# Attention gradients for one query: an eighth of the stores of V's gradient moved to GpSimd's DMA queue

## The chip, the cores and the metric

The kernel runs on one core of a Trainium2 chip. The metric is the device time of one execution in microseconds (us); the runs before the change have a median of 1301.13 us (three runs, 1300.45 to 1303.02). The core has five engines with their own instruction streams: TensorE (PE in the profile; its weight loads are PEld), VectorE (DVE), ScalarE (ACT), GpSimd (POOL) and SyncE (SP). Its 16 DMA engines move data between the device memory (HBM) and the on-chip memory (SBUF, 128 rows called partitions). A DMA is issued by SP, ACT or POOL and is split over the DMA engines; the profile names the queue by its issuer (SPq, ACTq).

## The reference: what is computed

For each of 2 x 32 heads there is one query q, and 8192 keys and values of 128 numbers, in bf16. The forward pass is

```
scores = q . k / sqrt(128);  p = softmax(scores);  out = sum of p * v
```

and the kernel returns `out` and the three gradients of it for a given `grad_out`: dq (as small as q), dk and dv (each as large as k and v, 134 MB). So 268 MB are read and 268 MB written, and there is little arithmetic for each byte. For one head, with dS = p * (grad_out . v - delta): dv is the outer product of p and grad_out, dk that of dS and q (scaled), and dq the sum of dS * k.

## The kernel before, in words

The 64 heads are handled as 32 pairs. K of a pair is one SBUF tile of 4 MB, [128 partitions, 128 positions, 128 numbers]; partitions 0 to 63 hold one head, 64 to 127 the other. V of the pair is another such tile. One partition is 32 KB of contiguous device memory.

There are six such buffers (`ring`, 24 MB), so three pairs are on the chip at a time. The gradients are written in place: once V of a pair is used up, dV (outer product of the row grad_out and the weights p) is written over V, and dK over K (`outer`, L275, on VectorE). Then the buffer is stored (`store`, L283, issued by ScalarE), and when the store has landed, SP loads K or V of the pair three later into it (`load`, L108). dV of pair g sits in the buffer that K of pair g+3 takes, and dK of g in the one that V of g+3 takes.

The order of all work is written out by hand. The outer loop runs over h, the pair that is being read in; the inner loop over 16 steps j, 8 chunks of K and then 8 of V. At each step TensorE transposes a chunk (L119), ScalarE or VectorE copies the result out (`ev`, L126 and L124), and TensorE multiplies it by the query or by grad_out (L136). Pair h-1 is finished in the same steps: its step number ("slot") is s = j + 16. In slots 12 to 17 dV is written, in slot 18 (j = 2 of the next pair) it is stored; in slots 19 to 23 dK is written and in slot 24 (j = 8) stored. Directly after each store's issue in program order stands the load of the pair three later, on SP's queue. SP works through its queue in order, and each load waits there for the store of its buffer to land. The last pair is stored in eight parts (1 MB each) as it is finished.

GpSimd does nothing in the loop: it prepares constants and clears two weight tiles (`wz`, L295) at the start. No DMA is issued by it.

Of the kernel before, what the change touches and what calls it, by code (L numbers as in the profile page):

```python
# [11 lines left out]
BF16 = mybir.dt.bfloat16  # L12
# [2 lines left out]
CH = 16  # L15
HC = CH // 2
RING = 6


@with_exitstack  # L20
def kernel(
# [11 lines left out]
    nc = tc.nc  # L33
    B, H, Sq, D = q.shape
    Sk = k.shape[2]
    P = nc.NUM_PARTITIONS
# [4 lines left out]
    NT = 2 * Sk // P  # L41
# [6 lines left out]
    const = ctx.enter_context(tc.tile_pool(name="const", bufs=1))  # L48
# [18 lines left out]
    q_rows = q.rearrange("b h s d -> (b h s) d")  # L67
# [4 lines left out]
    def by_pairs(x):  # L72
        rows = x.rearrange("b h s d -> (b h s) d")
        return rows.rearrange("(g p n) d -> g p n d", p=P, n=NT)

    k_v, v_v, dk_v, dv_v = (by_pairs(x) for x in (k, v, out_2, out_3))
# [8 lines left out]

    ring = [kvp.tile([P, NT, D], BF16, name=f"ring{i}") for i in range(RING)]
    acc = ps_one.tile([P, 4 * D], F32, name="acc", tag="acc")
# [12 lines left out]
    pairs = [Pair() for _ in range(NP)]  # L100
# [6 lines left out]
    def load(g, w):  # L107
        nc.sync.dma_start(out=pairs[g].kv[w][:], in_=(k_v, v_v)[w][g])  # L108
# [4 lines left out]
    def transposes(g, j, u):  # L113
        x = pairs[g]
        w, c = divmod(j, NCH)
        tp = ps_tp.tile([P, HC, P], F32, name="tp", tag="tp")
        for i in range(HC):
            n = c * CH + u * HC + i
            nc.tensor.matmul(  # L119
                tp[:, i, :], lhsT=x.kv[w][:, n, :], rhs=ident_bf[:], start=True, stop=True  # L120
            )
        ev = evp.tile([P, HC, P], BF16, name="ev", tag="ev")
        if (j, u) in ((8, 0), (9, 0), (10, 0), (11, 0)):
            nc.vector.tensor_copy(out=ev[:], in_=tp[:])  # L124
        else:
            nc.scalar.copy(out=ev[:], in_=tp[:])  # L126
        x.ev[j, u] = ev

    def products(g, j, u):
        x = pairs[g]  # L130
        w, c = divmod(j, NCH)
        ev = x.ev.pop((j, u))
        cols = (qT_all, doT_all)[w][:, 2 * g : 2 * g + 2]
        for i in range(HC):
            n = c * CH + u * HC + i
            nc.tensor.matmul(  # L136
                scores(w)[:, :, n], lhsT=ev[:, i, :], rhs=cols, start=True, stop=True
            )

    def spread_row(g, w):  # L140
        pb = misc[:, (2 + w) * D : (3 + w) * D]
        for s, hs in enumerate(halves):
            nc.tensor.matmul(  # L143
                pb[hs],
                lhsT=ident_bf[0:BH, 2 * g + s : 2 * g + s + 1].to_broadcast([BH, HP]),
                rhs=nat[:, 1 - w, :],
                start=True,
                stop=True,
            )
        x = pairs[g]  # L150
        x.row = rowp.tile([P, D], BF16, name="row", tag="row")
        nc.scalar.copy(out=x.row[:], in_=pb)  # L152

    def row_max(x):
        x.mp = work.tile([P, 1], F32, name="mp", tag="mp")
        for s, hs in enumerate(halves):
            nc.vector.reduce_max(out=x.mp[hs], in_=scores(0)[hs, s, :], axis=AX.X)  # L157

    def all_max(x):
        mT = sm[0:1, 2 * NT : 2 * NT + P]  # L160
        nc.tensor.transpose(mT, x.mp[:], ident_f[:])
        x.gm = work.tile([1, 2], F32, name="gm", tag="gm")
        nc.vector.reduce_max(out=x.gm[:], in_=mT.rearrange("o (s p) -> o s p", s=2), axis=AX.X)

    def exps(x):
        mb = sm[:, 2 * NT + P : 2 * NT + P + 2]
        nc.tensor.matmul(mb, lhsT=ones_row[:], rhs=x.gm[:], start=True, stop=True)  # L167
        negm = work.tile([P, 1], F32, name="negm", tag="negm")
        x.E = big.tile([P, NT], F32, name="E_f", tag="E_f")
        x.ld = work.tile([P, 2], F32, name="ld", tag="ld")  # L170
        for s, hs in enumerate(halves):
            nc.vector.tensor_scalar(
                out=negm[hs], in0=mb[hs, s : s + 1], scalar1=-scale, scalar2=None, op0=ALU.mult
            )
        for s, hs in enumerate(halves):
            nc.scalar.activation(  # L176
                out=x.E[hs],
                in_=scores(0)[hs, s, :],
                func=ACT.Exp,
                bias=negm[hs],  # L180
                scale=scale,
                accum_out=x.ld[hs, 0:1],
            )

    def sums(x, w):
        x.lsum = (dp if w else sm)[:, 2 * NT + P + 8 : 2 * NT + P + 9]
        nc.tensor.matmul(x.lsum, lhsT=block[:], rhs=x.ld[:, w : w + 1], start=True, stop=True)  # L187
# [72 lines left out]
    def combine(g):  # L260
        x = pairs[g]
        c = misc[:, 0:4]
        for j in range(4):
            nc.tensor.matmul(  # L264
                c, lhsT=x.accsb[:, j * D : (j + 1) * D], rhs=pick[:, j],
                start=(j == 0), stop=(j == 3),
            )
        nc.vector.tensor_copy(  # L268
            out=colsT[:, :, 2 * g : 2 * g + 2], in_=c.rearrange("p (w s) -> p w s", w=2)
        )  # L270

    def outer(x, w, c):
# [6 lines left out]
            op=ALU.mult,  # L279
        )  # L280

    def store(g, w, a=0, b=NT):
        nc.scalar.dma_start(  # L283
            out=(dv_v, dk_v)[w][g][:, a:b, :], in_=pairs[g].kv[1 - w][:, a:b, :]
        )

    def outer_and_store(g, w, c):
        outer(pairs[g], w, c)
        if g == NP - 1 and c % 2:
            store(g, w, (c - 1) * CH, (c + 1) * CH)  # L290

    for i, src in enumerate((q_rows, do_rows)):
        nc.scalar.dma_start(out=nat[:, i, :], in_=src)
    for t in wz:
# [12 lines left out]
    STORE = {18: 0, 24: 1}  # L307

    with tc.manual_schedule():
        for g in range(RING // 2):  # L310
            load(g, 0)
            load(g, 1)
        for h in range(NP + 1):
            y = pairs[h] if h < NP else None
            x = pairs[h - 1] if h else None
            for j in range(NS):
                at = [(z, zg, s) for z, zg, s in ((x, h - 1, j + NS), (y, h, j)) if z]
                for u in range(2):
                    if y:
                        transposes(h, j, u)  # L320
                    if y and j:
                        products(h, j - 1, u)
                    elif x and j == 0:
                        products(h - 1, NS - 1, u)
                    if u == 0:
                        if y and j == 8:
                            spread_row(h, 0)
                        if x and j == 2:
                            spread_row(h - 1, 1)
                        if x and j == 8:  # L330
                            combine(h - 1)
                    else:
                        if y and j == 9:
                            all_max(y)
                        if y and j == 10:
                            exps(y)
                        if y and j == 11:
                            sums(y, 0)
                        if x and j == 1:
                            sums(x, 1)  # L340
                    if u == 1:
                        for z, zg, s in at:
                            for w, when in ((0, ACC_V), (1, ACC_K)):
                                for c in when.get(s, ()):
                                    weighted_rows(z, w, c)
                if y and j == 8:
                    row_max(y)
                if y and j == 11:
                    weights_v(y)
                if x and j == 0:  # L350
                    deltas(x)
                if x and j == 1:
                    weights_k(x)
                for z, zg, s in at:
                    if s in STORE and zg < NP - 1:
                        store(zg, STORE[s])
                        if zg + 3 < NP:
                            load(zg + 3, STORE[s])
                    for w, when in ((0, OUT_V), (1, OUT_K)):
                        for c in when.get(s, ()):  # L360
                            outer_and_store(zg, w, c)
                if x and j == 6:
                    acc_to_sbuf(x)
        for w, dst in enumerate((o_rows, dq_rows)):
            tps = ps_tp.tile([BH, P], BF16, name="tps", tag="tp")
            nc.tensor.transpose(tps[:], colsT[:, w, :], ident_bf[:])
            rows = evp.tile([BH, D], BF16, name=f"rows{w}", tag="ev")
            nc.scalar.copy(out=rows[:], in_=tps[:])
            nc.scalar.dma_start(out=dst, in_=rows[:])


# [28 lines left out]
```

## Time and profile before

| what | before |
|---|---|
| runs, median (lowest to highest) | 1301.13 us (1300.45 to 1303.02) |
| the profiled execution's own time | 1301.66 us |
| its span (first to last instruction) | 1299.9 us |
| PE, DVE, ACT, POOL busy | 84%, 72%, 70%, 0% of the span |
| HBM read, written | 268.47 MB, 268.47 MB (413 GB/s over the span) |
| loads on SP's queue, stores on ACT's | 64 of 4 MB; 62 of 4 MB and 8 of 1 MB |

How to read it: the profile's page has a line for each engine with its busy share in 40 equal slices of the span, given as digits (9 is 90% or more); the line "DMA" is the mean busy share of the 16 DMA engines. The "chain that ended last" follows the last instruction back to whatever released it, step by step, and gives the shares of the span by engine and line. "SPq L108 <- DMA out_dram<-ring" means that SP's queue, at line 108, waited for a DMA that stores a ring buffer. For DMA issues the page gives the median time from issue to landing. The trace also holds, for each transfer, the times of the sixteen increments of its semaphore, and for each packet (a contiguous run that one DMA engine moves) its queue, start, duration and size, without the name of the DMA engine. A view by windows gives, for a stretch of time, the busy time of each engine, the granted TensorE clock, the DMA engines' share and the GB/s moved.

### The profile page before, as it was taken

What the parts mean: (1) busy time and instruction counts of PE and PEld (TensorE: products, weight loads), DVE (VectorE), ACT (ScalarE), POOL (GpSimd) and SP (SyncE); (2) the same over time, 40 slices, a digit from 0 to 9 for tenths busy, and PEclk for the clock granted to TensorE, in tenths of its full rate; (3) what the DMA queues carried; (4) which work ended last, traced back from release to release, by engine and by line L of the source; (5) the groups of instructions that cost most, each with busy time, mean ns of one, the idle gap of its engine ahead of it and who ended that gap; (6) DMA issues with size and microseconds to landing.
All of it is one profiled execution on the core that took longest, in us unless ns stands there. A gap on an engine that the chain in (4) does not pass through costs nothing.

```text
span 1299.9 us, 42160 instructions
## 1 busy us (share of the span) xinstructions
PE 1093.5 (84%) x19044; PEld 936.6 (72%) x19044; DVE 930.0 (72%) x1355; ACT 906.3 (70%) x1091; POOL 2.0 (0%) x10
## 2 busy tenths in 40 slices
PE   4999899988888889888888887898888988889883
PEld 3777787776777778777677776677677877778771
DVE  0888788767867677767786676776677666776775
ACT  4887778767866678757686576876578666786761
POOL 0000000000000000000000000000000000000000
PEclk9999989889988788868898688988788777887876
DMA  9999999999999999999999999999999999999986
GB/s 404 417 425 424 429 427 432 427 430 430 429 429 427 427 426 420 427 430 403 426 429 427 429 400 429 432 423 423 414 393 420 416 405 410 410 421 419 404 348 268
DMA packets 19796, 539.64 MB, mean 415 GB/s; under 512 B 2464, under 2 KB 2464, under 8 KB 2464
## 3 DMA queue, kind: packets, MB, share of 16 engines
q10 hardware_dynamic: 10400, 268.51, 49.0%
q1 hardware_dynamic: 9216, 268.44, 48.8%
q8 instruction: 149, 2.44, 0.7%
q14 instruction: 31, 0.25, 0.0%
HBM read 268.47 MB, written 268.47 MB: 413 GB/s over the span
## 4 chain that ended last, share of the span: by engine, by line
DMA 63%; PE 24%; ACT 7%; DVE 3%; issue 2%; ACTq 0%; SPq 0%; DVEq 0%
DMA ring<-in_v_dram 43%; DMA out_dram<-ring 19%; PE tp L119 15%; ACT ev L126 5%; PE misc L264 3%; PE dp L136 2%; PE acc L247 1%; DVE ring L275 1%; DMA nat<-in_grad_out_dram 1%; PE sm L136 1%; DVE ev L124 1%; PE sm L167 1%; ACT E_f L176 1%; ACT row L152 1%; PE sm L187 0%
## 5 line engine op out<-in xcount | busy, mean ns | idle before, releaser
L126 ACT CAST ev<-tp 128x1024 bf16<-128x1024 f32 x896 | 865.4, 1020 | 287.0 <-PE tp L119 273.4
L119 PE MATMUL tp<-ident_bf,ring 128*128 128x128 bf16 x8192 | 721.9, 240 | 148.7 <-DMA ring<-in_v_dram 73.8
L119 PEld LDWEIGHTS <-ring 128*128 128x128 bf16 x8192 | 581.3, 108 | 286.7 <-issue 189.6
L136 PEld LDWEIGHTS <-ev 128*128 128x128 bf16 x8192 | 338.3, 100 | 7.3 <-issue 5.7
L275 DVE TENSOR_TENSOR ring<-row,dS 128x2048 bf16<-128x2048 bf16 x256 | 298.9, 1220 | 41.7 <-PE acc L247 39.9
L275 DVE TENSOR_TENSOR ring<-row,P 128x2048 bf16<-128x2048 bf16 x256 | 300.2, 1221 | 36.8 <-PE acc L247 35.8
L124 DVE CAST ev<-tp 128x1024 bf16<-128x1024 f32 x128 | 156.7, 1225 | 135.1 <-PE tp L119 131.6
L136 PE MATMUL dp<-doT_all,ev 128*128 128x2 bf16 x4096 | 185.7, 167 | 2.2 <-issue 1.4
L136 PE MATMUL sm<-qT_all,ev 128*128 128x2 bf16 x4096 | 178.9, 165 | 3.8 <-issue 3.7
L247 PE MATMUL acc<-ring,wz 128*16 128x512 bf16 x2048 | 167.8, 396 | 3.2 <-DVE wz L191 2.3
L152 ACT CAST row<-misc 128x128 bf16<-128x128 f32 x64 | 18.1, 282 | 81.5 <-PE misc L143 74.8
L264 PE MATMUL misc<-pick,accsb 128*128 128x4 f32 x256 | 52.0, 326 | 17.5 <-ACT row L152 11.2
L264 PEld LDWEIGHTS misc<-pick,accsb 128*128 128x128 f32 x256 | 49.2, 286 | 23.2 <-ACT row L152 16.0
L247 PEld LDWEIGHTS <-wz 128*16 128x16 bf16 x2048 | 31.2, 86 | 11.0 <-issue 2.7
L218 DVE CUSTOM_DVE_ANT_0 dSu<-E_f,dp 64x128 f32<-64x128 f32 x64 | 18.3, 285 | 28.5 <-PE dp L136 28.0
L157 DVE TENSOR_REDUCE mp<-sm 64x1 f32<-64x128 f32 x64 | 18.5, 289 | 21.9 <-PE sm L136 21.2
L268 DVE CAST colsT<-misc 128x4 bf16<-128x4 f32 x32 | 5.1, 161 | 31.8 <-PE misc L264 31.8
L176 ACT ACTIVATE E_f<-sm,negm 64x128 f32<-64x128 f32 x64 | 23.2, 363 | 1.7
L236 DVE SCALAR_TENSOR_TENSOR dSu<-dp,negdelta,E_f 64x128 f32<-64x128 f32 x64 | 22.4, 350 | 2.2
L258 DVE COPY accsb<-acc 128x512 f32<-128x512 f32 x32 | 22.1, 692 | 2.0 <-PE acc L247 1.0
L191 DVE TENSOR_SCALAR wz<-dSu,rl 64x128 bf16<-64x128 f32 x64 | 18.1, 283 | 2.1
L191 DVE TENSOR_SCALAR wz<-E_f,rl 64x128 bf16<-64x128 f32 x64 | 18.1, 283 | 1.7
(42 smaller groups left out, 197.6 us busy)
## 6 DMA issues: line engine op xcount, KB each, us to landing
out_dram<-ring ACTq DMA_DIRECT2D x62, 4096.0 KB, 45.9
ring<-in_k_dram SPq DMA_DIRECT2D x32, 4096.0 KB, 27.6
ring<-in_v_dram SPq DMA_DIRECT2D x32, 4096.0 KB, 27.8
out_dram<-ring ACTq DMA_DIRECT2D x8, 1024.0 KB, 11.3
out_dram<-rows ACTq DMA_DIRECT2D x2, 16.0 KB, 9.7
nat<-in_q_dram ACTq DMA_DIRECT2D x1, 16.0 KB, 11.0
nat<-in_grad_out_dram ACTq DMA_DIRECT2D x1, 16.0 KB, 15.4
```

The lines of the kernel that those rows point to most:

```text
L119: nc.tensor.matmul(tp[:, i, :], lhsT=x.kv[w][:, n, :], rhs=ident_bf[:], start=True, stop=True)
L124: nc.vector.tensor_copy(out=ev[:], in_=tp[:])
L126: nc.scalar.copy(out=ev[:], in_=tp[:])
L136: nc.tensor.matmul(scores(w)[:, :, n], lhsT=ev[:, i, :], rhs=cols, start=True, stop=True)
L152: nc.scalar.copy(out=x.row[:], in_=pb)
L176: nc.scalar.activation(out=x.E[hs], in_=scores(0)[hs, s, :], func=ACT.Exp, bias=negm[hs], scale=scale, accum_out=x.ld[hs, 0:1],)
L191: nc.vector.tensor_scalar(out=wz[w][hs, :, 8 * w + 4 * s : 8 * w + 4 * s + 4], in0=src[hs].rearrange("p (m j) -> p m j", j=4), scalar1=s1[ ...
L236: nc.vector.scalar_tensor_tensor(out=x.dSu[hs], in0=scores(1)[hs, s, :], scalar=negdelta[hs], in1=x.E[hs], op0=ALU.add, op1=ALU.mult,)
L247: nc.tensor.matmul(acc[32 * g : 32 * g + 16, :], lhsT=wz[w][:, n // 4, :], rhs=rows[:, n : n + 4, :].rearrange("p n d -> p (n d)"), start= ...
L258: nc.vector.tensor_copy(out=x.accsb[:], in_=acc[:])
L264: nc.tensor.matmul(c, lhsT=x.accsb[:, j * D : (j + 1) * D], rhs=pick[:, j], start=(j == 0), stop=(j == 3),)
L275: nc.vector.tensor_tensor(out=x.kv[1 - w][:, n : n + CH, :].rearrange("p n (d t) -> p n d t", t=2), in0=row.unsqueeze(1).to_broadcast([P, ...
```

## The change

In pairs 1, 5, 9, ... 29 (`RELIEF`, 8 of 32) the store of dV in slot 18 is divided. Positions 64 to 127 of every partition (2 MB) are still stored by ScalarE in one DMA. Positions 0 to 63 (16 KB of each partition, 2 MB) are stored by GpSimd in 24 DMAs, each of a few partitions with a stride of 4 (`rows`): 11 partitions from 52, 4 from 0, 3 from 20, 8 from 96 and 4 from 32, for each of four offsets r, and partitions 16+r and 48+r together (`fifth`). Some are cut into runs of 8 KB, some are left at 16 KB (`max_dma_last_dim`). Between them GpSimd issues 11 small DMAs (`turn`) that read 4 numbers of some rows of q into a tile that nothing uses (`spare`); one more such DMA stands at the start and one at the end of the kernel. In program order the 35 DMAs stand before ScalarE's half of the store, and both before the load of the pair three later, which waits for all of them.

```diff
+RELIEF = range(1, 32, 4)
...
+    spare = const.tile([P // 8, 48], BF16)
+    turns = []
+
+    def turn(n):
+        i = 4 * (len(turns) % 12)
+        turns.append(n)
+        two = lambda t: t.rearrange("p (a b) -> p a b", a=2)
+        nc.gpsimd.dma_start(out=two(spare[0:n, i : i + 4]), in_=two(q_rows[0:n, 0:4]))
+
+    def store_by_fifteen(g):
+        dst, src = (t[:, 0 : NT // 2, :] for t in (dv_v[g], pairs[g].kv[1]))
+
+        def rows(lo, n, step=4, size=8192):
+            own = slice(lo, lo + step * (n - 1) + 1, step)
+            nc.gpsimd.dma_start(out=dst[own], in_=src[own], max_dma_last_dim=size)
+
+        def fifth(r):
+            rows(16 + r, 2, step=32)
+
+        for r in range(4):
+            if r == 1:
+                fifth(r)
+                turn(14)
+            rows(52 + r, 11)
+            rows(r, 4, size=16384)
+            if r == 0:
+                fifth(r)
+                turn(3)
+            elif r == 3:
+                turn(10)
+                fifth(r)
+                turn(9)
+            else:
+                turn(5)
+            rows(20 + r, 3)
+            if r == 2:
+                fifth(r)
+                turn(14)
+            rows(96 + r, 8)
+            rows(32 + r, 4, size=16384)
+            turn(5)
...
+    turn(5)
     for i, src in enumerate((q_rows, do_rows)):
         nc.scalar.dma_start(out=nat[:, i, :], in_=src)
...
                     if s in STORE and zg < NP - 1:
-                        store(zg, STORE[s])
+                        split = zg in RELIEF and STORE[s] == 0
+                        if split:
+                            store_by_fifteen(zg)
+                        store(zg, STORE[s], NT // 2 if split else 0)
                         if zg + 3 < NP:
                             load(zg + 3, STORE[s])
...
+        turn(11)
```

The lines of the kernel move down by 1 up to the new functions and by 45 to 50 behind them: `load` is L109, the small DMAs L292, GpSimd's pieces L299, `store` L328.

## The prediction, made before the result was known

> **What bounds it now.** I read the page's slices and queues first, then the chain, the sync engine's waits and issues, and last the landing and packet records of the trace.
>
> ```profile
> DMA  9999999999999999999999999999999999999986
> ...
> DMA 63%; PE 24%; ACT 7%; DVE 3%; issue 2%; ACTq 0%; SPq 0%; DVEq 0%
> ```
>
> The DMA engines are full in all slices but the last two; the chain that ended last is DMA for 63%. TensorE (84%), VectorE (72%) and ScalarE (70%) have gaps.
>
> ```profile
> SPq L108 <- DMA out_dram<-ring: 1174.6, 58, 50.7
> ```
> ```profile
> 594.92 0.33 SPq L108 DMA_DIRECT2D ring<-in_k_dram  x1
> 615.11 0.33 SPq L108 DMA_DIRECT2D ring<-in_v_dram  x1
> 635.49 0.33 SPq L108 DMA_DIRECT2D ring<-in_k_dram  x1
> 655.47 0.33 SPq L108 DMA_DIRECT2D ring<-in_v_dram  x1
> ```
> ```profile
> out_dram<-ring ACTq DMA_DIRECT2D x62, 4096.0 KB, 45.9
> ring<-in_k_dram SPq DMA_DIRECT2D x32, 4096.0 KB, 27.6
> ring<-in_v_dram SPq DMA_DIRECT2D x32, 4096.0 KB, 27.8
> ```
>
> SP waits for 1174.6 us until stores have landed; it then loads into the freed buffer. Alternate loads repeat every 40.55 us, the period of one pair. A store takes 45.9 us from issue to landing, a load of the same size 27.7. The landing records say why. A transfer counts as landed when its sixteen increments, one for each DMA engine, are in. For the dV store issued at 592.12 the first came at 608.37, the fifteenth at 618.10, the sixteenth at 635.37; the K load at 635.49 waited for that one. From 450 us to 1230 us nearly every store looks so: one increment 10 to 29 us behind the other fifteen. **One DMA engine is late**, and the kernel moves at its pace. In the packet records I followed the chain of packets that ends in that last increment, 1021.9 to 1039.7 us: loads and stores alternate, seven of each, mean 1.235 us and 1.311 us, where the median 32 KB packet takes 1.213. Sixteen of each make 40.7 us: the period.
>
> ```profile
> 100.13 1.05 PE misc L264 x8
> 134.85 1.05 PE misc L264 x8
> 170.59 1.16 PE misc L264 x8
> ...
> 603.82 1.05 PE misc L264 x8
> ...
> 644.81 1.87 PE misc L264 x8
> ...
> 684.97 1.87 PE misc L264 x8
> ```
>
> The same instruction of successive pairs, in the chain: 34.7 and 35.7 us apart while the first buffers last, 41.0 and 40.2 later. So the compute could go 5 us a pair faster.
>
> How fast are the other fifteen? Early on they run ahead of the late one, unhindered:
>
> ```profile
> 160.00:325.00 165.00, 144.86 (x2601) 124.03 (x2598) 127.36 (x181) 123.64 (x148) 0.00 (x0) 0.89 1.00 429
> ...
> 975.00:1180.00 205.00, 179.77 (x2989) 154.91 (x2986) 146.08 (x211) 141.96 (x171) 0.00 (x0) 0.80 1.00 415
> ```
>
> A pair is 539.64 MB / 32 = 16.86 MB, 1.054 MB an engine. The late engine moves that in 40.55 us, 26.0 GB/s. Of the 429 GB/s (last column) the fifteen have 403, 26.87 each: 39.2 us a pair. Later all sixteen fall to the late one's pace (415). The room is 1.35 us a pair.
>
> **The change, part by part.**
> *Removed:* in 8 pairs (1, 5, ... 29) half of the dV store leaves ScalarE's queue. ScalarE keeps one issue of 0.34 us, now 2 MB.
> *Moved:* those 2 MB go by GpSimd in 24 pieces by row. Rows 16-19 and 48-51, one sixteenth of the rows as one DMA engine has one sixteenth of a transfer, go in four pieces of two rows. I take it that these rows are the late engine's and that their new engines are others; no record of this trace names an engine. Then the late engine is spared 8 x 16 KB = 4 packets of 32 KB at 1.311 = 5.24 us per relieved pair; eight other engines get 16 KB each, half of 1.213 = 0.6 us.
> [...]
> *Added:* 11 tiny DMAs per relieved pair (80 rows, two runs of 4 bytes each), one at the start (5 rows) and one at the end (11); the last is issued after the pieces of pair 29 and lands long before the end. GpSimd is busy 2.0 us in all, so its issuing delays nobody directly; the first stands ahead of two memsets first needed at 41 us.
> Price of a tiny packet on a DMA engine: unknown for this queue. Nearest rows: 4 bytes 9 ns, 256 bytes 18 ns; the upper end is the smallest large packet, 8 KB, 309 ns. Each engine gets at most 35 completions and 22 runs, 57: between 0.5 and 17.6 us per relieved pair. I take 18 ns, the nearest in size: 1.0 us.
> *New waits:* in the built order each GpSimd DMA waits for the eighth before it to land; behind it stand the later pieces. The K load of pair g+3 (L109) waits for the last pieces and ScalarE's half, and behind it in SP's queue stand the V load of g+3 and all later ones. Pair 14's dV store: issued 592.12, landed 635.37; K load of pair 17 landed 663.06; its first transpose at 663.1. That is 71 us from store to use; on the fifteen engines a load takes 20.4 us (first increment of that load, 655.90). So the pieces have 50 us, 1.45 us each, before TensorE waits. I cost this at nothing: with eight under way at a time 35 DMAs are 4.4 groups, and the smallest transfers of this trace (16 KB, the outputs' rows) land in 9.7 us: 4.4 x 9.7 = 43 us. Bounds: 43 us (no loss) and 71 us (rival B). The orders of PE, DVE, ACT and SP are otherwise the same.
>
> **Sum.** Late engine: 40.55 - (5.24 - 1.0)/4 = 39.5 us a pair. The others: 39.2 + (0.6 + 1.0)/4 = 39.6. The pace falls from 40.55 to 39.6, 0.95 us, over the 29 pairs from the first relief to the last load: 27.5 us. Against the profiled execution (span 1299.9, its own time 1301.66): 1274.2; the median of the runs is 0.5 lower, so 1274. With the cheap end of a tiny packet 1271; if every pair kept all of the 1.35 us, 1262.
>
> **Rivals.**
> *B, the pieces hold back the loads: slower.* In the packet records the 4-byte completion of a transfer takes a turn of its own between packets of the other queue. If each of the 35 DMAs must post on the late engine, whose two queues are never empty, a turn costs 1.235 + 1.311 = 2.55 us. SP's queue there lasts some 51 us after the store (the load issued at 615.11 landed at 642.9): 20 turns; the other 15 wait behind stores alone, 1.31 each, 20 us. The pieces land after 71 us, 21 later than the 50 they have. TensorE regains 5 us a pair, 15 until the next but three; so a relieved pair loses 6 to 21 us, less 27.5 in all: between 1322 and 1442, midway 1382. It decides from a spacing of about 1.5 us. For it: the late engine is full. Against: once loads are held, the queues empty and turns shorten.
> [...]
> *C, the late engine isn't the one passed by.* It then keeps its load and gets 57 tiny packets (8 x 1.0 us) and perhaps 8 x 0.6: 1302 to 1314.
> *D, nothing to move to.* All engines are busy (DMA share 1.00 in both windows above); if the fifteen's pace of 415 is a common limit and not waiting, the relief only changes who carries the bytes: 1294 to 1302. For it: packets between 893 and 1176 us average 1.25 to 1.28 us on all engines; against it: 429 early with the same mix.
> [...]
>
> **Chances.** Forecast (1260 to 1294): 0.54. B 0.24, C 0.10, D 0.12. A difference under 0.2% (2.6 us) can't be told from none. Faster: 0.54 + 0.08 of D = 0.62. Same: 0.04 of D + 0.05 of C = 0.09. Slower: 0.24 + 0.05 = 0.29. Range 1260 to 1335: below lies some 0.04, above most of B, 0.15.
>
> **What would show it.** Right: the sixteenth increment of the stores falls within some 10 us of the fifteenth, stores land in 25 to 35 us, GB/s near 425 in the middle, chain lines 39.6 us apart. B: SP's waits on GpSimd's pieces over 50 us, slices of DMA under 9 in every fourth pair, long TensorE waits for in_k. C: one increment as late as before. D: no late increment, yet 415 GB/s. Wrong above all if a tiny packet costs more than 74 ns: then 57 of them undo 4.2 of the 5.24 us.

## The result and the profile after

The changed kernel takes 1362.93 us (median of four runs, 1361.72 to 1365.69), the kernel before 1301.31 us on the same chip; the ratio is 1.0475 (95% interval 1.0455 to 1.0494). The forecast was 1274, faster; it went the other way, by 61.6 us, beyond the range. The profiled execution took 1363.45 us, its span is 1361.3. Where some executions of a kernel fell into a slower state of the chip, the times below are of the others.

The DMA slices and the chain, from the page of the changed kernel:

```profile
DMA  9998899996999969999699996999969999699998
GB/s 401 427 416 347 360 428 427 423 426 277 422 429 425 423 281 413 427 431 426 269 424 430 424 424 279 414 428 431 425 279 418 428 426 426 275 425 428 424 427 338
...
PE 12%; DMA 12%; ACT 5%; DVE 3%; issue 1%; POOL 1%; ACTq 0%; SPq 0%; DVEq 0%
```

Before, all slices but the last two were full. Now there are seven holes: two slices of 8 near the start, and then every fifth slice a 6, at 269 to 281 GB/s. The slices between are full, most of them at 413 to 431. Eight pairs are relieved. SyncE's queue shows the hole after the second relieved pair (the columns are start, duration, engine, line, transfer):

```profile
236.97 0.33 SPq L109 DMA_DIRECT2D ring<-in_k_dram  x1
258.10 0.33 SPq L109 DMA_DIRECT2D ring<-in_v_dram  x1
322.16 0.33 SPq L109 DMA_DIRECT2D ring<-in_k_dram  x1
322.65 0.33 SPq L109 DMA_DIRECT2D ring<-in_v_dram  x1
323.15 0.33 SPq L109 DMA_DIRECT2D ring<-in_k_dram  x1
323.59 0.42 SPq L109 DMA_DIRECT2D ring<-in_v_dram  x1
```

Before, a load went out every 20 us. Here none goes out for 64 us and then four at once: the first waited for the pieces, the other three, half a microsecond apart, stood behind it in the queue and then had nothing of their own to wait for. GpSimd's queue in that time (in brackets the idle time ahead of an issue, and what ended it):

```profile
245.48 1.72 POOL L299 DMA_DIRECT2D out_dram<-ring  x3 [103.70 <-DVE ring L276]
247.19 0.52 POOL L292 DMA_DIRECT2D spare<-in_q_dram  x1
247.71 1.70 POOL L299 DMA_DIRECT2D out_dram<-ring  x3
249.40 0.55 POOL L292 DMA_DIRECT2D spare<-in_q_dram  x1
257.18 0.58 POOL L299 DMA_DIRECT2D out_dram<-ring  x1 [7.23 <-DMA out_dram<-ring]
261.42 0.52 POOL L292 DMA_DIRECT2D spare<-in_q_dram  x1 [3.66 <-DMA out_dram<-ring]
266.87 0.60 POOL L299 DMA_DIRECT2D out_dram<-ring  x1 [4.93 <-DMA out_dram<-ring]
...
312.79 0.54 POOL L292 DMA_DIRECT2D spare<-in_q_dram  x1 [3.52 <-DMA out_dram<-ring]
314.22 1.12 POOL L299 DMA_DIRECT2D out_dram<-ring  x2 [0.89 <-DMA out_dram<-ring]
315.33 0.54 POOL L292 DMA_DIRECT2D spare<-in_q_dram  x1
```

Eight DMAs go out at once; from then on each waits, up to 8 us, for the one eight places ahead to land. By the landing records they land one behind the other: the first at 256.90, 11.4 us after its issue, the second at 261.14, the eighth at 290.48, 45.0 us after the first issue. The ninth goes out at 257.18, the 23rd at 312.79: one every 4.0 us. Then the other queues are empty, and the last twelve go out in 7 us. The K load follows at 322.16, 76.7 us after the first piece was issued, as soon as the last has landed.

What it does to the engines, by windows (the last three columns: granted clock, DMA share, GB/s):

```profile
160.00:243.00 83.00, 72.23 (x1280) 61.89 (x1281) 60.41 (x92) 60.58 (x73) 0.00 (x0) 0.85 1.00 427
245.00:325.00 80.00, 60.86 (x1070) 51.85 (x1068) 53.07 (x73) 51.12 (x61) 19.47 (x35) 0.81 0.86 359
325.00:413.00 88.00, 71.86 (x1274) 61.65 (x1275) 60.09 (x91) 60.24 (x72) 0.00 (x0) 0.82 1.00 427
```

In the 80 us with the hold the DMA engines stand idle for 0.14 x 80 = 11.2 us. Four pairs, from held load to held load (322.2 to 1175.0 us, five cycles), take 170.6 us; before, the same loads (272.0 to 1081.1) took 161.8. The difference is 8.7 us, and seven such holds make 61 of the 61.6 us: the whole loss. The eighth relieved pair, 29, has no load behind it. Of the 11.2 us idle 2.5 are won back: without them four pairs take 159.4 us, 39.9 a pair, where 40.5 were needed before.

TensorE pays where rival B put it, in the wait for K, which had been 5.2 us in all:

```profile
PE tp L120 <- DMA ring<-in_k_dram: 144.4, 7, 25.3
```

Its wait for V falls from 73.8 to 4.8 us, so that it waits 70 us more in all.

And the chain of the changed kernel names the new path, here in the sixth relieved pair (start, duration):

```profile
931.71 41.21 DMA spare<-in_q_dram
973.20 23.20 DMA out_dram<-ring
...
1004.54 12.10 DMA ring<-in_k_dram
1035.92 1.05 PE misc L265 x8
1071.16 1.05 PE misc L265 x8
```

Small DMAs and pieces for over 64 us, then a K load that needs only 12.1 us since nothing else moves, then a pair every 35 us, the compute's own pace, until the next hold.

### The profile page after: what moved, and what is told of

The parts are those of the page before. It is cut to its first block, busy times and chain, and to the rows that moved or that the text cites. A ratio compares the mean times of both kernels' runs of the same rounds, so it can differ in the third digit from the quotient of the medians.

```text
span 1361.3 us, 42484 instructions
## 1 busy us (share of the span) xinstructions
PE 1079.6 (79%) x19044; PEld 921.6 (68%) x19044; DVE 925.5 (68%) x1355; ACT 908.7 (67%) x1091; POOL 159.1 (12%) x292
## 5 line engine op out<-in xcount | busy, mean ns | idle before, releaser
L299 POOL DMA_DIRECT2D out_dram<-ring x192 | 109.7, 575 | 1061.3 <-DVE ring L276 755.4
L292 POOL DMA_DIRECT2D spare<-in_q_dram x90 | 48.0, 533 | 126.5 <-DMA out_dram<-ring 117.6
L265 PE MATMUL misc<-pick,accsb 128*128 128x4 f32 x256 | 36.2, 265 | 17.5 <-ACT row L153 11.1
L265 PEld LDWEIGHTS misc<-pick,accsb 128*128 128x128 f32 x256 | 33.4, 204 | 22.7 <-ACT row L153 15.5
## 6 DMA issues: line engine op xcount, KB each, us to landing
out_dram<-ring POOLq DMA_DIRECT2D x32, 176.0 KB, 12.1
```

Of the source, the lines that this page charges most:

```text
L265: nc.tensor.matmul(c, lhsT=x.accsb[:, j * D : (j + 1) * D], rhs=pick[:, j], start=(j == 0), stop=(j == 3),)
L292: nc.gpsimd.dma_start(out=two(spare[0:n, i : i + 4]), in_=two(q_rows[0:n, 0:4]))
L299: nc.gpsimd.dma_start(out=dst[own], in_=src[own], max_dma_last_dim=size)
```

## Experiments

The theory after the result, H: 35 DMAs, eight under way, each complete only after turns behind 32 KB packets on full engines, hold back the loads. The rival, E: GpSimd's stores and pieces cost the DMA engines their time themselves. Separate from both: does the relief work at all? Each kernel is compared with the kernel before on its own chip.

### What holds the loads: the number of DMAs

**Two pieces for 24, one for 24.** In the changed kernel the body of `store_by_fifteen` is replaced:

```
e1:  rows(0, 120, step=1); turn(2); rows(120, 8, step=1); turn(7)
e3:  rows(0, 128, step=1)
```

> The same 2 MB in the same 8 pairs, but in two GpSimd DMAs of 120 and 8 rows with two small ones (2 and 7 rows) between, 4 DMAs instead of 35. Theory H (the 35 DMAs, eight under way at a time, each complete only when all sixteen engines have posted, hold back the loads for 76 us): with 4 DMAs the pieces land in 40 to 50 us, the loads are not held, and the relief shows: 1270 to 1285 us. Theory E (a GpSimd store costs its DMA engines more than ScalarE's, whatever the number of pieces): the time stays near 1362. Theory R (the late engine gains nothing from being passed by): 1300 to 1310.

> In the same 8 pairs GpSimd stores the same 2 MB in one DMA of all 128 rows, which uses all sixteen engines: GpSimd's queue without pieces and without relief. Theory H: no loss and no gain, one engine late as before: 1299 to 1305 us. Theory E: slower by several us a relieved pair, 1320 or more.

e1: 1309.17 us, ratio 1.0058 (1.0031 to 1.0085). e3: 1302.77, ratio 1.0016 (0.9983 to 1.0048), no change that can be measured. The page's DMA issues of e3 (KB each, median us to landing):

```profile
out_dram<-ring POOLq DMA_DIRECT2D x8, 2048.0 KB, 43.7
```

The same 2 MB in one GpSimd DMA land in 43.7 us instead of 76.7. E falls: neither GpSimd's queue nor the division between it and ScalarE has a cost that can be measured. e1 still loses 7 us with four DMAs, the last landing 52 to 63 us after its issue in the pairs from the second on.

**Half the bytes.** The pieces take positions 0 to 31, ScalarE the other 96; still 35 DMAs, with runs of half the length (4 and 8 KB). Its first change:

```diff
-        dst, src = (t[:, 0 : NT // 2, :] for t in (dv_v[g], pairs[g].kv[1]))
+        dst, src = (t[:, 0 : NT // 4, :] for t in (dv_v[g], pairs[g].kv[1]))
```

> The 35 DMAs of the change in the same 8 pairs, each with half the bytes (positions 0 to 31; ScalarE stores the other 96). Theory H by number of DMAs: the pieces still take 65 to 75 us, the relief is half: 1350 to 1380 us. Theory H by bytes (16 turns of 8 KB an engine are what takes the time): the pieces take about half, and the time falls to 1300 to 1320 us.

1375.58 us, ratio 1.0561 (1.0541 to 1.0582): half the bytes in pieces, and slower than the changed kernel. The K load behind the second relieved pair goes out 75.9 us after the first piece (247.7 to 323.6), as in the changed kernel. Bytes don't set the landing. From the second relieved pair on, the loads stand still for 65.7 us on average instead of 63.9; why a little longer stays open.

**Small DMAs alone.** The stores of the kernel before; GpSimd issues 35 small DMAs for each of the eight pairs. No store or load waits for them and they wait for none, so that they go out one after another up to 1148 us, not pair by pair.

> All stores as before the change; GpSimd issues the same number of DMAs (35 for each of 8 pairs), each small: 4 numbers of as many rows, so that no store is done by them and no load waits for them. They measure the price of completions and small packets alone. Theory H: at most 1 us a relieved pair: 1300 to 1309 us. Theory E: 1330 us or more.

1307.86 us, ratio 1.0044 (1.0028 to 1.006): 0.7 us a relieved pair. Its GpSimd queue, in the middle of the kernel, gives the price of a DMA while both other queues stay full:

```profile
258.55 0.52 POOL L292 DMA_DIRECT2D spare<-in_q_dram  x1 [3.11 <-DMA spare<-in_q_dram]
263.39 0.52 POOL L292 DMA_DIRECT2D spare<-in_q_dram  x1 [4.32 <-DMA spare<-in_q_dram]
267.17 0.52 POOL L292 DMA_DIRECT2D spare<-in_q_dram  x1 [3.26 <-DMA spare<-in_q_dram]
271.88 0.52 POOL L292 DMA_DIRECT2D spare<-in_q_dram  x1 [4.19 <-DMA spare<-in_q_dram]
```

Most go out 3.6 to 4.9 us apart, three or four times the 1.21 us of a 32 KB packet, though each moves less than 0.2 KB; each lands after 35 us, seven others being ahead of it. This is the row that the trace of before lacked: 35 at this pace would take some 150 us. In the changed kernel they take half as long because eight start at once and the held loads empty the queues at the end.

**Fewer DMAs, the same pieces.** The changed kernel without the eleven small DMAs in a relieved pair: 24 DMAs.

> The changed kernel without the 11 small DMAs in each relieved pair: the same 24 pieces, 24 DMAs instead of 35 (the two small ones at the start and end stay; which engines the pieces take is given up). If the number of DMAs, eight under way at a time, sets when the last piece lands, it lands after 24/35 of 76 us = 52 us, about the 50 that a load can be held at no cost, and a relieved pair loses 0 to 2 us: 1301 to 1317. If the bytes in small pieces do it: 76 us as before and 1362.

1333.69 us, ratio 1.0235 (1.0204 to 1.0267): half the loss is gone. My figure of 52 us to landing was wrong. It is 73.5:

```profile
242.89 4.46 POOL L299 DMA_DIRECT2D out_dram<-ring  x8 [115.42 <-DVE ring L276]
254.27 0.57 POOL L299 DMA_DIRECT2D out_dram<-ring  x1 [6.92 <-DMA out_dram<-ring]
257.96 0.56 POOL L299 DMA_DIRECT2D out_dram<-ring  x1 [3.12 <-DMA out_dram<-ring]
...
313.30 0.55 POOL L299 DMA_DIRECT2D out_dram<-ring  x1 [3.42 <-DMA out_dram<-ring]
314.11 0.55 POOL L299 DMA_DIRECT2D out_dram<-ring  x1 [0.26 <-issue]
```

Its ninth to 24th go out 4.0 us apart (254.27 to 314.11), as in the changed kernel, where the first 23 took 67 us as well; only the last twelve, in emptied queues, were cheap. So the landing isn't proportional to the number: a DMA costs 4 us while the queues are full and 0.6 after. K loads are 166.1 us apart in four pairs, 4.2 above before, times seven: 30. SyncE's loads stand still for 59.4 us in a hold instead of 63.9, and the rest of the four pairs takes the same 106.7 us in both kernels.

**Packets are a better count than DMAs.** By the packet counts in the last section each DMA puts on every engine one packet for its completion and as many as a sharing engine has runs: two for a small DMA or a piece with uncut rows, three for a piece cut into 8 KB runs. The first eight DMAs of a hold are 20 such packets in the changed kernel and 21 in e16. The eighth lands 45.0 us after the first issue in the one (second relieved pair) and 46.3 in the other: some 2.2 us a packet. In e8, with two packets each, DMAs land 4.4 us apart on average, again 2.2. The single DMA of e3, 17 packets, takes 43.7 us, 2.6 each. The estimate that fits all four is 2.2 to 2.6 us for each packet of GpSimd's on an engine that two full queues share, near the turn of 2.55 us of rival B.

**The pieces where no load waits.** The 35 DMAs only in pair 29, with no load behind it (`RELIEF = (29,)`).

> The change's 35 DMAs unaltered, only in pair 29, where no load waits for them and the kernel's end is still far off (pieces issued about 1200, landed about 1276). Theory H: nothing held, the late engine spared 5.2 us: 1295 to 1302 us. Theory E (each relieved pair costs 7.7 us by itself): 1307 to 1311 us.

1300.99 us, ratio 0.9986 (0.9968 to 1.0004). The pieces take longer than ever, the first issued at 1195.1 us, the last at 1282.3; nothing waits for them, and they cost nothing. With e3 this decides for H: it is the wait of the loads, not the work of the pieces. An earlier try went astray:

> The 35 DMAs of the change, unaltered, but only in pairs 29 and 30, whose buffers are not loaded again, so that no load waits for them. Theory H: nothing is held back; the late engine is spared twice 5.2 us near the end: 1291 to 1302 us. Theory E (the pieces cost the engines their time themselves, 7.7 us a relieved pair as measured over 8): 1301 + 15 = 1316 us.

1316.33 us, 1.0121 (1.0093 to 1.0148): in pair 30 the kernel's own end waits for the pieces (SyncE's last wait, 82.7 us, is for one of them), so it says nothing on E.

**Earlier pieces.** If the hold is the price, an earlier issue should help:

```diff
+                    if s == 14 and zg in RELIEF:
+                        store_by_fifteen(zg)
```

> The change with its 35 DMAs unaltered, but issued after slot 14 instead of 18, as soon as positions 0 to 63 of dV are written: about 10 us earlier. Theory H (the pieces' landing, 76 us after issue, holds the loads): each relieved pair loses up to 10 us less: 1285 to 1310 us. Theory E (the pieces cost the engines their time, wherever they stand): 1355 to 1365 us.

1530.85 us, 1.1758 (1.1732 to 1.1784), far off, for a reason that I had not seen. VectorE now waits for the pieces:

```profile
DVE ring L276 <- DMA spare<-in_q_dram: 344.9, 8, 52.3
```

The rest of dV is written into the tile that the pieces read, and the program as built makes its next write wait for them. The test of the earlier issue is spoilt. With two pieces instead of 24 this wait doesn't arise:

> The two pieces of 120 and 8 rows (4 DMAs a relieved pair, landed 56 us after issue in the run of two pieces at slot 18), issued after slot 14. Theory H: they now land within the 50 us that the K load can wait, nothing is held, and the relief of the late engine shows: 1270 to 1285 us. Theory R (no relief in it): 1300 to 1310 us.

1311.71 us, 1.0067 (1.0047 to 1.0087), no better than e1.

### The relief

**Which engine is late.** A scan: the kernel before, and behind the dV store of six pairs a copy on ScalarE's queue that gives k engines 4 packets of 32 KB each.

```
BURDEN = {8: 4, 12: 5, 16: 8, 20: 12, 24: 15, 28: 16}      # pair: k
dst, src = (t.rearrange("(a b) n d -> a b n d", b=8)[0:k, 0:4] for t in (dv_v[NP - 1], k_v[0]))
nc.scalar.dma_start(out=dst, in_=src, max_dma_last_dim=32768)
```

> The kernel before, with one copy from device memory to device memory behind the dV store of pairs 8, 12, 16, 20, 24 and 28, on ScalarE's queue: 4 packets of 32 KB for each of k engines, k = 4, 5, 8, 12, 15, 16 in that order (rows of K of pair 0 into dV of pair 31, overwritten later by the store of that pair). Which engine is late: four packets on the late engine cost it 4 x 1.24 to 1.31 = 5 us, on another engine nothing, since the other fifteen run 1.35 us a pair faster. So a pair's period (40.55 us) grows once by 5 us at each copy that the late engine has part in. If a copy of k parts goes to the first k engines and the late one is the fifth, as the change takes it to be: 0 at k = 4, 5 us at each of the other five, 1326 us in all. If it is one of the first four: all six, 1331. If it is the sixth to eighth: from k = 8, 1321; ninth to twelfth: 1316; the last: k = 16 alone, 1306. [...]

1330.02 us, 1.0202 (1.0181 to 1.0223): 27 us more, for 25 expected. SyncE's loads, around the copy of pair 8 (the K load at 392.99 waits for that pair's dV store) and of pair 12 (554.44):

```profile
392.99 0.33 SPq L109 DMA_DIRECT2D ring<-in_k_dram  x1
...
433.23 0.33 SPq L109 DMA_DIRECT2D ring<-in_k_dram  x1
...
554.44 0.33 SPq L109 DMA_DIRECT2D ring<-in_k_dram  x1
583.46 0.33 SPq L109 DMA_DIRECT2D ring<-in_v_dram  x1
600.90 0.33 SPq L109 DMA_DIRECT2D ring<-in_k_dram  x1
620.60 0.33 SPq L109 DMA_DIRECT2D ring<-in_v_dram  x1
640.91 0.33 SPq L109 DMA_DIRECT2D ring<-in_k_dram  x1
```

After k = 4 the K loads stay 40.2 to 40.4 us apart. After k = 5 they are 86.5 us apart in two pairs, 5.4 more than 81.1; the same step comes at 8, 12 and 15 (86.0 to 86.5 us). At 16, where no K load is left, the V load goes out 29.2 us behind the K load, as at the others. So **the late engine has a part in the copies of 5 parts and more, and none in the copy of 4**. In that order it is the fifth, and the engines of the copy of 4 are the first four; below the names mean no more than this. Which row of a store an engine moves, the scan doesn't show. Four packets on the late engine cost the kernel 5.4 us (86.5 for 81.1), and as many on each of the first four, at k = 4, nothing.

**Do GpSimd's DMAs go round?** Eight copies of two parts on GpSimd's queue.

> The kernel before, with one copy from device memory to device memory at slot 18 of pairs 8, 10, ... 22, on GpSimd's queue: two parts, each of 8 packets of 32 KB. If each such DMA takes the next two of the sixteen engines in turn, as the change's small DMAs suppose, the eight copies go once round: exactly one of them burdens the late engine, with 8 x 1.24 to 1.31 = 10 us, and a pair's period grows by 10 us there and nowhere else; the time is 1311 us. If the order starts at the first engine and the late one is the fifth, it is the copy of pair 12. If GpSimd's copies always take the same two engines, there is no step or there are eight: 1301 or 1381 us.

1315.35 us, 1.0107 (1.0071 to 1.0143): 12 us, one burden of 10, not none and not eight. But a copy waited only for the one ahead of it, and all eight were issued by 212 us, not pair by pair, so no step can be read off. The landings of the first loads show part of it: after the first copy two increments of sixteen are some 9.5 us behind the fourteen others, after the second four, after the third six. So the two parts of a copy go to two engines, and the next copy's to two others. Which copy burdened the fifth isn't shown.

**Another engine passed by.** The changed kernel with `turn(9)` at the start and `turn(7)` at the end.

> The changed kernel with 9 rows instead of 5 in the small DMA at the start and 7 instead of 11 at the end: if the order of GpSimd's parts goes on from DMA to DMA, another engine is passed by than in the changed kernel. If the relief does nothing there, because the engines stand idle for 11 to 12 us while a load is held, more than the 4 x 1.35 us by which the late one falls behind in four pairs: the same as the changed kernel, 1362 within 4 us. If the relief was worth the 5.24 us that I gave it: 8 x 5.24 = 42 us more, 1400.

1365.8 us, 1.0489 (1.0453 to 1.0525) against 1.0475 (1.0455 to 1.0494): the same. With these row counts the start makes no difference that can be measured.

**Relief without a hold.** Six kernels tried to spare the fifth engine with few DMAs. e7 is e6 with the start and end of e15. e9 to e11 store all of dV in two pieces (120 and 8 rows, as e1): in pair 29 alone, the same with the other start, and in pairs 1, 9, 17, 25.

> As the two pieces at slot 14, with the same DMAs, but the small DMA at the start has 9 rows instead of 5 (and the one at the end 7 instead of 11), so that the fifteen engines, if a cursor sets them, are others and another engine than the late one is passed by. If the relief is real and the late engine is the fifth: no relief, 20 to 30 us slower than the two pieces at slot 14, about 1300 to 1312. If no engine is singled out (theory R): the same time as those.

> Only pair 29's dV, whole (4 MB), goes by GpSimd in two pieces of 120 and 8 rows with the small DMAs as before (5 rows at the start). Its buffer is not loaded again, so no load waits for the pieces; the last K and V loads still stand behind the late engine's queue. If the relief is real and the late engine sets the pace (theories H and E agree): it is spared 8 packets, 10.5 us: 1289 to 1296 us. Theory R (passing by the fifth engine gives nothing): 1300 to 1305 us.

> The same two pieces in pair 29, but the small DMA at the start has 9 rows (7 at the end), so that another engine is passed by. If the late engine is the fifth and the small DMAs set the engines: no relief, 1300 to 1305 us, some 10 us above the run with 5 rows. If the number of rows at the start does not matter: the same as that run.

> Whole dV of pairs 1, 9, 17, 25 in the two pieces: the same bytes pass by the late engine as in the change, with half as many pairs in which a load waits for GpSimd's pieces, in 16 KB runs. Theory H: 4 times a few us of held loads against a relief of up to 27 us: 1280 to 1300 us. Theory R: 1305 to 1315 us.

e7: 1312.96 us, 1.0078 (1.006 to 1.0095), the same as e6. e9: 1316.46, 1.0127 (1.0088 to 1.0166); e10: 1314.8, 1.0109 (1.0077 to 1.0142); e11: 1325.49, 1.0177 (1.0128 to 1.0226). No gain, and no difference by the start. In e9 and e10 the dK store ahead of pair 29's pieces lands after 59 to 60 us instead of 49.2: the last engine has more to do, not less. The packet counts show that 120 rows went to fifteen engines (last section). The packet records show that the late engine was one of them. An engine's packets can be followed back from its last increment, since in full queues each starts 3 or 4 ns before the recorded end of the one ahead of it. In e10 the chain that ends in that store's last increment holds eight 16 KB packets of GpSimd's queue between 1203.9 and 1234.8 us, in e9 at least two (1227.43 and 1230.53). So on this chip the engine left out was not the late one, at either start, and these runs can't price the relief. The scan ran on another chip; whether the late engine is the fifth on each of them wasn't looked at.

e1 did take the lag away: the sixteenth increment of its stores comes 2.0 us behind the fifteenth on average, 14.6 before, while the DMA engines stay full on the whole (share 1.00 from 231 to 1040 us). Yet TensorE waits as long for V as before (73.6 us for 73.8), and the time isn't shorter. In e3, with all sixteen engines in use, the lag falls too, to 5.2. So a smaller lag alone is no sign of a gain; why it shrinks stays open.

The last two are meant to put the extra rows on the first four engines, which the scan had found free; that four rows of a store go where the four parts of the copy went is my assumption. e17, every fourth pair: rows 0 to 111 in one ScalarE DMA, 112 to 127 in four of 4 rows. e18, every second pair: rows 0 to 111 by ScalarE, 112 to 122 in one GpSimd DMA with a small one of 5 rows behind it, 123 to 126 and 127 by ScalarE.

> The kernel before; in pairs 1, 5, ... 29 the dV store goes by ScalarE alone in five DMAs: rows 0 to 111 in one (7 rows for each engine), rows 112 to 127 in four of 4 rows. If 4 rows go to the first four engines, as the copies of 4 parts did in the scan (no step at k = 4, one at k = 5), the fifth is spared one row of 1.31 us in such a pair, the first four get three more, 3.6 us. Late engine: 40.55 - 1.31/4 = 40.22 us a pair; the first four: 39.2 + 3.6/4 = 40.1. 0.33 us over 29 pairs is 9.5 us: 1293, ratio 0.993. If the relief gives nothing (a common limit): 1303, or a few us more for 32 further DMAs.

> The kernel before; in every second pair (1, 3, ... 29) the dV store goes as rows 0 to 111 by ScalarE, rows 112 to 122 by GpSimd in one DMA of 11 parts, rows 123 to 126 by ScalarE (first four engines), row 127 by ScalarE (first engine). [...] Two GpSimd DMAs a pair instead of 35, so no load is held. If the piece passes by the fifth: late engine 40.55 - 1.31/2 = 39.9 us a pair, the first 39.2 + 1.2/2 = 39.8: 0.65 x 29 = 19 us less, 1284, ratio 0.985. If GpSimd's 11 rows take the first eleven engines each time, the fifth is not relieved: 1303 to 1306.

e17: 1335.34 us (1328.79 to 1348.02), 1.0287 (1.0234 to 1.0339). e18: 1347.26 (1339.85 to 1357.27), 1.0351 (1.0304 to 1.0397). Both slower, and the traces show costs that I had not counted. ScalarE's queue in e17:

```profile
407.56 11.13 ACTq L290 DMA_DIRECT2D out_dram<-ring  x5
418.79 1.93 ACT L127 CAST ev<-tp 128x1024 bf16<-128x1024 f32 x2 [11.60 <-DMA out_dram<-ring]
```

Five issues took 11.1 us instead of 5 x 0.34: as built, the fourth waits for an earlier transfer to land, and ScalarE's next copy for TensorE stands behind it. In e18 the single row is what the K load at 456.7 waits for: issued at 405.2 us, it landed at 456.5; and in the DMA of 4 rows ahead of it one increment is 18 us behind the other three. Both fit one engine, that of the single row, as the new late one, at 42.2 us a pair (K loads at 286.3 and 1130.3, twenty pairs apart) where I had worked out 39.8. That it is one of the four, with one row more, is inferred from that increment; why it is so much slower, and which engines the eleven rows took, stays open. No version beat the kernel before.

## Why the prediction was wrong

**What bounds the kernel: right.** One DMA engine is late, and on the chip of the scan it is the one with a part from k = 5 on (e13, 27 us for 25 worked out).

**The relief, 5.24 us a relieved pair: a second step that failed.** In the changed kernel the sixteenth increment of a store comes 1.0 us behind the fifteenth on average; before, it was 14.6. That was my sign of success, and it is none: in every hold the engines idle for 9 to 11 us, more than the 4 x 1.35 = 5.4 by which the late one falls behind in four pairs, so it can catch up relieved or not. The term itself rests on an assumption: that rows 16 to 19 and 48 to 51 are the late engine's and that the pieces take them to others. No run shows the term. Nor does the supposition on record for e14 give it, that GpSimd's DMAs take the engines in turn, here one a row (the two, four and six late increments of its first copies agree with that): by it, wherever the turn starts, every engine gets 6 to 10 of the 128 rows of the 24 pieces, where 8 would be its plain share. I had not added that up. In place of the term e12 showed no relief. With the same 35 DMAs the late engine of that chip was not spared: the chain that ends in the last increment of the store issued at 1213.6 us holds two 8 KB packets of GpSimd's queue, at 1249.59 and 1251.18. e12, with one relieved pair and no hold, gains at most 4 us by its interval (0.3%). What steering would be worth, done right, stays open.

**Tiny packets, 18 ns: too dear, and harmless.** A packet of 4 bytes of this queue took 9 ns (median), and so did one of 8, as which a row of a small DMA goes. An engine gets 72 of both for a relieved pair, not 57: 0.65 us. e8 puts all of them at 0.7 us a relieved pair, near my 1.0.

**The new waits, "I cost this at nothing": the step that failed.** It held two figures. The budget, 50 us from issue to landing before TensorE waits, was right: 76.7 - 50 = 26.7, and TensorE waits up to 25.3 us. The landing, "4.4 x 9.7 = 43 us", measured 76.7. The sum lets eight DMAs land together in the time of one. For one the 9.7 us, although taken from the emptied queues at the end of the kernel, were near: the first piece of a hold lands after 11.4 us amid full queues. But the eight land one behind the other, and the eighth 45.0 us after the first issue. So the overlap was wrong, and not the row: GpSimd's next DMAs go out 4.0 us apart, against a bound of 1.45 that I had worked out myself.

**Rival B: right in its place, and in its size partly by luck.** It said 71 us to landing; it was 76.7. It gave each of the first 20 one turn of 2.55 us; in fact each puts two or three packets on an engine, and after 67 us 15 had landed. It gave the other 15 some 20 us; the last 20 landed within 10. The two errors nearly cancel. The point against it, that turns shorten once loads are held, came true too late: for the last twelve. It charged 6 to 21 us a relieved pair; it was 8.7, seven times, not eight, and the 27.5 us of relief that it took off did not appear. What supports it best was in my own text: the engines are full, so a completion on them takes turns. I gave it 0.24 and let the range stop at 1335, inside its 1322 to 1442.

B's condition, that each of the 35 DMAs posts on the late engine, fits the landing records: the 282 GpSimd DMAs of the changed kernel, of 2 to 14 rows each, made 4512 increments, sixteen each. The packet counts agree (last section).

**C and D** are not told apart in the changed kernel: the holds hide the late engine. e12 has C's condition, a late engine that isn't passed by. D's common limit of 415 GB/s is refuted: between the holds 427 move over 88 us.

## What to carry to other kernels

Before you divide a number of DMAs by how many may be under way, ask whether these land together or one behind the other: here the first landed after 11.4 us and the eighth after 45. Where a transfer is cut into many DMAs, multiply their spacing in full queues by their number and hold it against the time in which a buffer must come free; and count what stands behind the waiting load in the same queue. A hold can also remove the very sign that you meant to read, so find the condition in which the benefit would show alone before trusting it. And where a change rests on a rule of distribution, add up by the rule what each engine gets.

## What the runs showed of the hardware

- **An engine that a piece passes by is not free of it.** The packets of 4 bytes on GpSimd's queue fit one rule to the last one: 16 for each DMA, and on each engine without a share as many as an engine with a share moves runs. A piece of 11 rows in two runs makes 16 + 5 x 2 = 26, the copy of two parts with 8 runs 16 + 14 x 8 = 128. The sums are 8624 in the changed kernel, 6448 in e16, 1000 in e1, 843 in e18, 1024 in e14, as counted. The same rule shows that 11 rows went to eleven engines and 120 to fifteen.
- **A small packet is short, but its turn is long.** It takes 9 ns; DMAs of such packets in e8 mostly go out three or four times 1.21 us apart, the time of a 32 KB packet. That each waits for such packets of the other queues is inferred from this spacing.
- **A 4 MB load takes 12.1 us on idle engines and 27.7 among stores.** After a hold four loads go out at once, and a gap of 64 us in the loads costs 8.7 us.
- **One DMA engine of sixteen is some 3% slower than the rest** (40.55 us for a pair's share, against an estimate of 39.2 for the others). In the scan, on one chip, it has a part in the copies from k = 5 on; what makes it slow no run shows.
